# The float16 low half of g: a negated copy and an accumulating transfer on GpSimd's queue in place of VectorE's subtraction

## The chip, the cores and the metric

The kernel runs on one core of one Trainium2 chip. The metric is the device time of that core, in microseconds, and the median of several executions is taken. The core has TensorE (PE: matmuls, and PEld: the loads of their weights), VectorE (DVE), ScalarE (ACT), GpSimd (POOL) and SyncE (SP), each with its own instruction stream in a fixed order. SP and POOL also issue DMA transfers, each on its own queue.

## The reference

The input is a linear attention with 8 batches, 8 heads, 576 rows and a head size of 64, followed by a two-layer block over all 4608 rows:

```python
q_s = softmax(q, axis=-1); k_s = softmax(k, axis=2)      # written out with max, exp and sum
kv = np.einsum('bhsd,bhse->bhde', k_s, v)
x = np.einsum('bhsd,bhde->bhse', q_s, kv)                # then to rows: 4608 x 512
h = x @ w_in                                             # 512 x 2048
sp = np.maximum(h, 0.0) + np.log1p(np.exp(-np.abs(h)))
g = h * erf(sp)
out = g @ w_out                                          # 2048 x 512
```

w_in and w_out come as 64-bit floats and are rebuilt on the chip.

## The kernel before

**Tiles and items.** The rows are cut into blocks of 384 (12 blocks: four pairs of batches, three blocks each), and the 2048 inner columns into four groups of 512. One block with one group is an item; there are 48, n = 0 to 47. The items 0 to 3 run wholly in float32, and 4 and 5 (`OUT32`) have a float32 second product. The 42 items from 6 on use float16 pairs: a number is a float16 high half and the float16 rest.

**An item's steps.** `mm1` makes h in TensorE: the product with w_in by a scheme of seven half-size products, banks X, Y and Z, line 911. VectorE and ScalarE gather the banks into the tile H (128 x 4 x 384 float32, three buffers). ScalarE writes softplus of H into G (two buffers), and erf of G over G. `gmul` (line 991) makes g = G times H in G. From there H is free for other use: its bytes are read as two float16 tiles, gh in the first half and gl in the second. `ghi` (line 1005) casts g to gh, and `glo` (line 1009) writes g - gh to gl. `mm2` (line 1037) multiplies g with w_out on TensorE: for each of three row tiles and four quarters it takes gh with the high weights, gh with the low weights, and gl with the high weights, 36 matmuls of 128 x 512 with a weight load from H each. The sum of a block's four items is scaled by VectorE (line 1053) and stored from SP's queue.

**The order.** A table and the loop behind it write the steps down; a scheduler may still shift instructions of an engine against each other. In the loop, iteration n has the softplus and erf of item n at its end, and `gmul` of item n-1 at its start:

```python
        for i in range(4):
            if m0:
                tok(f"m{n}.{i}")
            if 4 < n <= N and i < 2 and n - 1 not in OUT32:
                tok(f"{'IO'[i]}{n - 1}")
            ...
            if m2 and i < 3:
                tok(f"M{n - 2}.{i}")
                pace(n + (i + 1) / NTT)
```

Here m is `mm1`, I is `ghi`, O is `glo` and M is `mm2`. So the halves of item n-1 are made in iteration n, between the products of item n, and are used one iteration later, after `m{n+1}.0`. `pace` puts pieces of the attention of later batches (lines 435 to 720) between them.

**Queues.** SP issues the loads of q, k and v and all stores. POOL issues the later weight loads (line 188), clears the tile vtail once for each batch (lines 432 and 433), and does little else.

Of the kernel before, what the change touches and what calls it, by code (L numbers as in the profile page):

```python
# [13 lines left out]
ALU = mybir.AluOpType  # L14
# [42 lines left out]
def attn_moe_kernel(  # L57
# [9 lines left out]
    nc = tc.nc  # L67
# [898 lines left out]
    def flat(t):  # L966
        return t.rearrange("p f t -> p (f t)")
# [38 lines left out]

    def glo(n):
        s = st[n]
        nc.vector.tensor_tensor(flat(s["gl"]), flat(s["G"]), flat(s["gh"]), op=ALU.subtract)  # L1009

    acc = {}

# [44 lines left out]

    steps = start()
    fn = dict(T=softplus, G=erf, U=gmul, I=ghi, O=glo)
    emitted_steps = set()  # L1060
    done = set()
# [127 lines left out]
```

## Time and profile before

| what | value |
|---|---|
| median of three runs | 862.84 us (860.36, 862.84, 862.9) |
| span of the profiled execution | 860.3 us; the run nearest to it took 860.36 us |
| TensorE busy | 825.6 us, 96% of the span |
| VectorE busy | 637.1 us, 74% |
| ScalarE busy | 504.2 us, 59% |
| GpSimd busy | 17.6 us, 2% |
| line 1009, the subtraction | 42 times, 73.8 us on VectorE |
| mean granted clock of TensorE | 0.989 |

No time of the profiled execution beside its span is listed apart. In a row of groups stand line, engine, operation, written tile <- read tiles, shapes and count; then busy time and the mean of one in ns; then the idle time of the engine ahead of them and what ended it. In a row of the timeline stand start, duration, engine, line and operation, and in brackets how long the engine sat idle before it and for whom. A busy time is that of the whole group with overlaps counted once, so one matmul of line 1037 occupies TensorE for 348.0 / 1512 = 0.23 us although its own duration is 379 ns.

### The profile page before, as it was taken

How to read it: one execution, taken by the hardware profiler on the slowest of the kernel's cores; microseconds unless marked ns; L12 is line 12 of the kernel's file. 1: busy time of each engine (PE TensorE's matmuls, PEld its weight loads, DVE VectorE, ACT ScalarE, POOL GpSimd, SP SyncE). 2: the span in 40 equal slices, each digit the busy share in tenths (PEclk: the TensorE clock that was granted, in tenths of full speed). 3: DMA queues.
4: the chain of work that ended last, by engine and by line, in shares of the span. 5: the costliest groups of instructions: out<-in, count | busy, mean ns of one | idle time of the engine just before them, and what ended most of it. 6: DMA issues, size and time to landing. Idle time of an engine off the chain costs nothing.

```text
span 860.3 us, 15503 instructions
## 1 busy us (share of the span) xinstructions
PE 825.6 (96%) x6532; PEld 569.2 (66%) x6532; DVE 637.1 (74%) x921; ACT 504.2 (59%) x645; POOL 17.6 (2%) x37
## 2 busy tenths in 40 slices
PE   3999997999999999999999999999999999999997
PEld 2655556676766776776776677767776677777673
DVE  6899889998886779759866779858866656653543
ACT  2597677866554566565664466466655466453532
POOL 2010000000000000000000000000000000000000
PEclk8999999999999999999999999999999999999999
DMA  9996320032123302311140202311110000100100
GB/s 273 397 268 178 100 75 13 19 88 50 37 54 77 87 1 50 93 28 24 50 105 14 68 19 51 80 38 26 32 32 2 25 13 2 37 2 1 37 2 37
DMA packets 117381, 55.53 MB, mean 65 GB/s; under 512 B 106560, under 2 KB 108608, under 8 KB 117312
## 3 DMA queue, kind: packets, MB, share of 16 engines
q1 hardware_dynamic: 115136, 46.15, 20.6%
q0 software_dynamic: 2176, 8.39, 2.7%
q8 instruction: 51, 0.84, 0.4%
q14 instruction: 18, 0.15, 0.1%
HBM read 45.09 MB, written 9.44 MB: 63 GB/s over the span
## 4 chain that ended last, share of the span: by engine, by line
PE 67%; DVE 17%; ACT 10%; issue 2%; DMA 2%; SPq 1%; POOL 0%; ACTq 0%; DVEq 0%; POOLq 0%
PE o L1037 31%; PE pX L911 16%; PE pZ L911 8%; ACT G L343 4%; PE pY L911 4%; ACT L343 3%; PE kv L541 2%; DVE G L991 2%; PE x L631 2%; PE qT L616 2%; DVE H L1009 1%; DVE x L297 1%; PE o L1028 1%; DVE wi L297 1%; DVE H L1005 1%
## 5 line engine op out<-in xcount | busy, mean ns | idle before, releaser
L1037 PE MATMUL o<-wo,H 128*128 128x512 f16 x1512 | 348.0, 379 | 1.7 <-DVE H L1005 1.3
L911 PEld LDWEIGHTS <-wi 128*128 128x128 f16 x3696 | 309.5, 98 | 39.0 <-issue 17.4
L1037 PEld LDWEIGHTS <-H 128*128 128x128 f16 x1512 | 145.7, 98 | 150.1 <-DVE H L1005 1.8
L911 PE MATMUL pX<-x,wi 128*128 128x192 f16 x2112 | 204.8, 247 | 6.4 <-ACT H L930 3.0
L343 ACT ACT_TABLE_LOAD x104 | 133.4, 1283 | 8.5 <-DVE H L936 5.3
L991 DVE SCALAR_TENSOR_TENSOR G<-G,small,H 128x1536 f32<-128x1536 f32 x44 | 80.0, 1818 | 65.8 <-ACT G L343 65.5
L911 PE MATMUL pZ<-x,wi 128*128 128x192 f16 x1056 | 102.9, 246 | 0.9 <-DVE H L936 0.5
L938 ACT COPY H<-pX 128x384 f32<-128x384 f32 x44 | 20.9, 476 | 138.0 <-PE pX L911 133.0
L343 ACT ACTIVATE G<-H,U 128x768 f32<-128x768 f32 (+1 forms) x60 | 72.9, 1231 | 24.4 <-DVE H L936 23.8
L1009 DVE TENSOR_TENSOR H<-G,H 128x1536 f16<-128x1536 f32 x42 | 73.8, 1757 | 1.1
L343 ACT ACTIVATE G<-G 128x1536 f32<-128x1536 f32 x48 | 71.2, 1484 | 0.5
L1028 PE MATMUL o<-wo,G 128*128 128x512 f32 x144 | 66.7, 604 | 0.0
L911 PE MATMUL pY<-x,wi 128*128 128x192 f16 x528 | 51.8, 248 | 1.6 <-DVE H L923 1.6
L442 ACT ACTIVATE x<-x 128x384 f32<-128x384 f32 (+1 forms) x52 | 17.6, 386 | 54.4 <-PE x L631 51.9
L923 DVE COPY H<-pY 128x384 f32<-128x384 f32 x44 | 24.4, 554 | 31.4 <-PE pY L911 31.3
L1028 PEld LDWEIGHTS o<-wo,G 128*128 128x128 f32 x144 | 26.3, 193 | 26.5 <-issue 25.8
L297 DVE SCALAR_TENSOR_TENSOR x<-x,x 128x768 f16<-128x768 f32 (+1 forms) x44 | 37.1, 850 | 5.8 <-ACT x L296 5.7
L1005 DVE CAST H<-G 128x1536 f16<-128x1536 f32 x42 | 40.1, 955 | 0.7
L296 ACT ACTIVATE x<-x 128x768 f16<-128x768 f32 (+1 forms) x44 | 32.9, 761 | 11.4 <-DVE x L387 11.4
L1053 DVE TENSOR_SCALAR ob<-o,V 128x512 f32<-128x512 f32 x29 | 21.7, 748 | 23.1 <-PE o L1037 23.1
L936 DVE TENSOR_TENSOR H<-pZ,H 128x384 f32<-128x384 f32 x44 | 24.3, 552 | 19.3 <-PE pZ L911 19.3
L925 DVE TENSOR_TENSOR H<-pX,H 128x384 f32<-128x384 f32 x44 | 24.4, 555 | 15.3 <-PE pX L911 14.9
(182 smaller groups left out, 804.2 us busy)
## 6 DMA issues: line engine op xcount, KB each, us to landing
out_dram<-ob SPq DMA_DIRECT2D x32, 256.0 KB, 2.3
vbuf<-in_v_dram SPq DMA_DIRECT2D x60, 128.0 KB, 3.1
q<-in_q_dram SPq DMA_DIRECT2D x56, 128.0 KB, 3.2
k<-in_k_dram SPq DMA_DIRECT2D x56, 128.0 KB, 3.3
wo<-in_moe_w_in_dram SPq DMA_DIRECT2D x4, 1024.0 KB, 16.9
wi<-in_moe_w_out_dram POOLq DMA_DIRECT2D x2, 1024.0 KB, 8.3
wi<-in_moe_w_in_dram SPq DMA_DIRECT2D x2, 1024.0 KB, 8.0
raw<-in_moe_w_out_dram POOLq DMA_DIRECT2D x2, 1024.0 KB, 7.9
```

What stands on the lines that cost most here:

```text
L296: nc.scalar.activation(hi, src, AF.Copy, scale=s)
L297: nc.vector.scalar_tensor_tensor(lo, src, s, hi, op0=ALU.mult, op1=ALU.subtract)
L343: i = nc.scalar.activation(out_, in_, func, **kw)
L911: nc.tensor.matmul(o, w[wl][:, c, a * P:(a + 1) * P], x[:, xl, xi, c, :], start=(new and a == 0 and c == 0 and i == 0), stop=(c == 1 and i ...
L923: nc.vector.tensor_copy(C[0, 0], bank2("Y"))
L925: add(C[0, 0], bank2("X"), C[0, 0], op=ALU.add)
L936: add(C[0, 1], bank2("Z"), C[0, 1], op=ALU.add)
L991: nc.vector.scalar_tensor_tensor(flat(s["G"]), flat(s["G"]), (GB if n in OUT32 else GA)[:, g:g + 1], flat(s["H"]), op0=ALU.mult, op1=ALU.mult,
L1005: nc.vector.tensor_copy(flat(s["gh"]), flat(s["G"]))
L1009: nc.vector.tensor_tensor(flat(s["gl"]), flat(s["G"]), flat(s["gh"]), op=ALU.subtract)
L1028: nc.tensor.matmul(o, s["G"][:, a, ts_], w[:, a, :], start=(first_ and a == 0), stop=(last_ and a == FG - 1),)
L1037: nc.tensor.matmul(o, s[gt][:, a, ts_], w[wl][:, a, :], start=(first_ and a == 0 and i == 0), stop=(last_ and a == FG - 1 and i == 2),)
```

## The change

VectorE no longer subtracts. It writes gl = -1 times gh, from float16 to float16, and a transfer on GpSimd's queue reads g from G and adds it to gl in place, with g in float32 and gl in float16. The instruction behind `glo` is thereby a transfer; whoever reads gl waits for its landing, and who overwrites G or H waits for it too.

```diff
     def glo(n):
         s = st[n]
-        nc.vector.tensor_tensor(flat(s["gl"]), flat(s["G"]), flat(s["gh"]), op=ALU.subtract)
+        nc.vector.tensor_scalar_mul(flat(s["gl"]), flat(s["gh"]), -1.0)
+        nc.gpsimd.dma_start(flat(s["gl"]), flat(s["G"]), accum_op=ALU.add)
```

All later lines move down by one: the matmuls of line 1037 are line 1038 after the change. In the rows below, the number in a tile's name is that of its item or batch, `o_4_0` and the like are the three row tiles of a block's sum, and a wait on DMASW is a wait for a transfer of GpSimd's queue.

TensorE at item 6, the first with a float16 low half, before: the loads and matmuls of the high half, then the first of the low half.

```order
L1037 LDWEIGHTS H_6_1142 [waits DVE_49]
L1037 MATMUL o_4_0_1176<-wo4_97,H_6_1142 128x512 [waits DMASW7_49]
...
L1037 MATMUL o_4_1_1232<-wo4_97,H_6_1142 128x512
...
L1037 MATMUL o_4_2_1285<-wo4_97,H_6_1142 128x512
L1037 LDWEIGHTS H_6_1142 [waits DVE_49]
```

And with the change:

```order
L1038 LDWEIGHTS H_6_1142 [waits DVE_49]
L1038 MATMUL o_4_0_1176<-wo4_97,H_6_1142 128x512 [waits DMASW7_49]
...
L631 MATMUL x_2_0_1561<-qTs_2_0_1481,kvbd0_85 128x512 [waits DVE_49]
L631 LDWEIGHTS kvbd0_85 [waits DVE_49]
L631 MATMUL x_2_0_1561<-qTs_2_0_1481,kvbd0_85 128x512
L616 MATMUL qT_2_1_1569<-ident_76,q_2_0_741 128x128 [waits DMAHW5_49]
L616 MATMUL qT_2_1_1569<-ident_76,q_2_0_741 128x128 x3
L911 LDWEIGHTS wi0_89
L911 MATMUL pZ_8_1582<-x7_2_1171,wi0_89 128x192 [waits DVE_49]
...
L1038 LDWEIGHTS H_6_1142 [waits DMASW0_49]
```

Two of the six matmuls on the high half have gone behind the wait; three matmuls of line 631, four transposes of line 616 and twelve pZ matmuls of line 911 stand ahead of it now.

TensorE at item 47, the last, with the change; before, the same rows stand in the same order, and the second wait is on DVE alone beside ACT's.

```order
L1038 LDWEIGHTS H_47_8366 [waits DVE_49]
L1038 MATMUL o_44_0_8255<-wo2_95,H_47_8366 128x512
...
L1038 MATMUL o_44_1_8297<-wo2_95,H_47_8366 128x512
...
L1038 MATMUL o_44_2_8323<-wo2_95,H_47_8366 128x512
L1038 LDWEIGHTS H_47_8366 [waits DMASW1_49,Activation_49]
```

Six matmuls stand between the two waits, before and after. In the 40 items between, the wait for the transfer stands on the load before the third matmul.

GpSimd's queue with the change; before, the rows of line 432 and 433 stand there alone.

```order
L1010 DMA H_9_1713<-G_9_1877 128x1536 [waits DMASW0_49,DVE_49,DMASW3_49,PE_49,Activation_49]
L1010 DMA H_10_1881<-G_10_2096 128x1536 [waits DVE_49,DMASW1_49,PE_49,Activation_49]
L432 MEMSET vtail_84 64x520 [waits DMAHW6_49,PE_49,Pool_49]
L433 MEMSET vtail_84 64x8
L1010 DMA H_11_2100<-G_11_2309 128x1536 [waits DMASW2_49,DMASW5_49,DVE_49,Activation_49]
```

The 42 transfers stand in order of their items, and the clears for four of the batches stand between them.

## The prediction

> **What bounds the kernel now.** I read the page's busy shares first, then its 40 slices, then TensorE by stage, then the waits around the two instructions that the diff touches.
>
> ```profile
> span 860.3 us, 15503 instructions
> PE 825.6 (96%) x6532; PEld 569.2 (66%) x6532; DVE 637.1 (74%) x921; ACT 504.2 (59%) x645; POOL 17.6 (2%) x37
> PE   3999997999999999999999999999999999999997
> ...
> 600.00:760.00 160.00, 158.61 (x1360) 113.31 (x1358) 105.40 (x142) 90.35 (x105) 0.00 (x0) 1.00 0.06 19
> 760.00:845.00 85.00, 85.00 (x673) 58.75 (x671) 37.10 (x41) 40.16 (x41) 0.00 (x0) 1.00 0.03 10
> ```
>
> The last two rows are two stretches: length, then busy time of PE, PEld, DVE, ACT and POOL, clock, DMA share. TensorE is busy for 85.00 of 85.00 us and 158.61 of 160.00: it is the bound, and VectorE (37.10 of 85.00) is far from it. Time that VectorE saves is worth only what it takes out of TensorE's waits, and these are few:
>
> ```profile
> L1009 DVE TENSOR_TENSOR H<-G,H 128x1536 f16<-128x1536 f32 x42 | 73.8, 1757 | 1.1
> L1005 DVE CAST H<-G 128x1536 f16<-128x1536 f32 x42 | 40.1, 955 | 0.7
> ...
> PE pX L911 <- DVE H L933: 2.1, 4, 0.7
> PE xt L631 <- DVE qTt L610: 2.1, 2, 1.0
> PE o L1037 <- DVE H L1005: 1.3, 1, 1.3
> PE o L1037 <- DVE H L1009: 0.4, 1, 0.4
> ```
>
> The subtraction (L1009) takes 42 times 1.757 us, and TensorE waited for it once, 0.4 us. That is the last item, where nothing is left to hide it:
>
> ```profile
> 846.60 0.96 DVE L1005 CAST H<-G 128x1536 f16<-128x1536 f32 x1
> 847.59 1.76 DVE L1009 TENSOR_TENSOR H<-G,H 128x1536 f16<-128x1536 f32 x1
> 847.61 1.47 PE L1037 MATMUL o<-wo,H 128*128 128x512 f16 x6 [1.33 <-DVE H L1005]
> 849.49 6.63 PE L1037 MATMUL o<-wo,H 128*128 128x512 f16 x30 [0.41 <-DVE H L1009]
> 856.17 0.75 DVE L1053 TENSOR_SCALAR ob<-o,V 128x512 f32<-128x512 f32 x1 [1.41 <-PE o L1037]
> ```
>
> Six matmuls need only the high half; the other 30 stand behind the first use of the low half. So whatever comes later than 849.46 there is added to the end.
>
> **How much cover the other 41 have.** I paired each L1009 with the first weight load of its low half. TensorE's order gives two loads of the high half and then one of the low half; a group of three loads takes 0.40 us and one load 98 ns, so the low half is wanted 0.30 us after a group's start.
>
> ```profile
> 198.36 0.40 PEld L1037 LDWEIGHTS <-H 128*128 128x128 f16 x3
> ...
> 192.40 1.74 DVE L1009 TENSOR_TENSOR H<-G,H 128x1536 f16<-128x1536 f32 x1
> 194.20 1.84 PEld L1037 LDWEIGHTS <-H 128*128 128x128 f16 x10 [0.35 <-DVE H L1009]
> ...
> 408.20 1.75 DVE L1009 TENSOR_TENSOR H<-G,H 128x1536 f16<-128x1536 f32 x1
> 413.36 1.04 PEld L1037 LDWEIGHTS <-H 128*128 128x128 f16 x6
> ...
> 732.19 1.75 DVE L1009 TENSOR_TENSOR H<-G,H 128x1536 f16<-128x1536 f32 x1
> 736.36 1.04 PEld L1037 LDWEIGHTS <-H 128*128 128x128 f16 x6
> ...
> 818.19 1.76 DVE L1009 TENSOR_TENSOR H<-G,H 128x1536 f16<-128x1536 f32 x1
> 825.55 2.34 PEld L1037 LDWEIGHTS <-H 128*128 128x128 f16 x12
> ...
> 832.89 1.76 DVE L1009 TENSOR_TENSOR H<-G,H 128x1536 f16<-128x1536 f32 x1
> 838.27 7.52 PEld L1037 LDWEIGHTS <-H 128*128 128x128 f16 x36
> ```
>
> Cover, from the start of L1009 to the want: item 6 has 194.20 - 192.40 = 1.80 us; item 19 has 413.66 - 408.20 = 5.46; item 39 has 4.47; item 45 has 7.66; item 46 has 5.68; item 47 has 849.46 - 847.59 = 1.87. The 42 pairs, worked out alike and sorted: 1.80, 1.87, 4.47, 5.46, 5.46, 5.67, 5.91, 6.12, 6.18, 6.18, then 32 from 7.23 to 10.20 us.
>
> **The change part by part.** Removed: 42 subtractions. Added on VectorE: 42 multiplications by -1, f16 to f16. The trace has none. Its bounds are 0.347 us, a tensor-scalar of 256 elements that writes f16, and the CAST's 0.955, which has the same 1536 elements and the same output but reads four bytes each. I take 0.95, as the CAST is nearest.
>
> ```profile
> L594 DVE TENSOR_SCALAR kvbd<-kvf,x_s 64x256 f16<-64x256 f32 x12 | 4.2, 347 | 0.2
> ```
>
> The Trainium skill ("VectorE: DVE Perf Modes", section "Mode 4×_2P — both tricks at once") has a one-source operation on packed 16-bit data in SBUF run at four elements a cycle. The CAST's 955 ns fits its two-a-cycle mode (1536 / 2 / 0.96 GHz = 800 ns and some 155 ns), and by the rule the multiplication would take an estimated 0.56 us; the stalls below would then sum to about 13.4 us in place of 17.0.
>
> Added behind it: 42 accumulating transfers on GpSimd's queue, g (128 x 1536 f32, 0.75 MB) onto -gh in place (0.375 MB, read and written). The nearest rows are GpSimd's weight loads of 1 MB:
>
> ```profile
> 69.28 0.71 POOL L188 DMA_DIRECT2D raw<-in_moe_w_out_dram  x1 [7.14 <-DVE wo L215]
> DMA to landing us min/median/max: 5.3/8.4/22.0
> ```
>
> From issue to landing the fastest of line L188 takes 5.3 us; the others share the DMA engines with other loads. Lower bound: 5.3 x 0.75 = 4.0 us, if only g's bytes count. Upper bound: 10.6, if each row passes the engine twice, once to read and once to add. I take 5.3 x 1.125 = 6.0 us, by bytes read (0.75 + 0.375 MB), since the loads' rows also pay for reading and writing together. So the low half is ready 0.95 + 6.0 = 6.95 us after the place where L1009 started, against 1.757 now.
>
> The Trainium skill ("DMA: Bandwidth & Descriptors", section "Anatomy of one DMA — SWDGE (gpsimd) path") puts such a transfer at 2.0 us and bytes / 436e3: an estimated 3.8 us for 0.79 million bytes. The row speaks against it: 1 MB would be 4.4, and the trace's best is 5.3. By it the stalls would come to 4.0 us.
>
> **The sum.** An item stalls TensorE by 6.95 less its cover, less the stall of the item before: ScalarE and VectorE start item n from its mm1, which stands ahead of item n-1's stalled mm2, so a stall there gives item n as much more cover.
> - Item 6: the new order puts other work ahead of the want: three L631 matmuls (19.9 / 72 = 0.28 each), four L616 transposes (0.155), twelve pZ matmuls (102.9 / 1056 = 0.097), two of its own fewer (348.0 / 1512 = 0.23): 0.83 + 0.62 + 1.17 - 0.46 = 2.16 us. Stall 6.95 - 3.96 = 2.99.
> - Items 8, 13, 19, 25, 31, 37, 39, 46: 0.83 + 0.77 + 1.49 + 0.77 + 1.49 + 1.04 + 2.48 + 1.28 = 10.15.
> - Item 47: 6.95 - 1.87 - 1.28 = 3.80.
> - Together 16.9 (17.0 unrounded).
>
> ```profile
> L631 PE MATMUL x<-qTs,kvbd 128*128 128x512 f16 x72 | 19.9, 379 | 0.2 <-DVE qTs L610 0.2
> L616 PE MATMUL qT<-ident,q 128*128 128x128 f32 x128 | 19.9, 283 | 0.0
> L911 PE MATMUL pZ<-x,wi 128*128 128x192 f16 x1056 | 102.9, 246 | 0.9 <-DVE H L936 0.5
> L1037 PE MATMUL o<-wo,H 128*128 128x512 f16 x1512 | 348.0, 379 | 1.7 <-DVE H L1005 1.3
> ```
>
> Taken back: 42 x (1.757 - 0.95) = 34 us of VectorE, of which TensorE sees what it waited for behind L1009. Those are L933's 2.1 us in four waits; the two shown stand just ahead of the wants of items 8 and 39, which stall now, so what they give is lost there, and about 1 us is left.
>
> ```profile
> 224.75 1.15 PE L911 MATMUL pX<-x,wi 128*128 128x192 f16 x12 [0.48 <-DVE H L933]
> ...
> 734.46 1.15 PE L911 MATMUL pX<-x,wi 128*128 128x192 f16 x12 [0.29 <-DVE H L933]
> ```
>
> At no cost: GpSimd's queue. Behind the waiting transfers stand four clears of vtail; the first ran at 257.11, right beside an L1009 at 256.89, and would now go after that item's issue, 256.89 + 0.95 + 0.71 = 258.55, some 1.5 us late. The next was released 88 us later, so the batch has room; were that gone, 4 x 1.5 us would show. The reverse, a transfer held by a clear that waits for TensorE, I price at nothing too: these clears were released 0.2 and 3.2 us after the L1009 ahead of them (256.89, 342.55), while the next L1009 comes about an item, some 15 us, later.
>
> ```profile
> 256.89 1.76 DVE L1009 TENSOR_TENSOR H<-G,H 128x1536 f16<-128x1536 f32 x1
> 257.11 0.53 POOL L432 MEMSET vtail<- 64x520 f32 x1 [79.78 <-PE kv L541]
> 342.55 1.75 DVE L1009 TENSOR_TENSOR H<-G,H 128x1536 f16<-128x1536 f32 x1
> 345.78 0.52 POOL L432 MEMSET vtail<- 64x520 f32 x1 [87.98 <-PE kv L541]
> ```
>
> Reuse of G is free as well: softplus overwrites it two items later, and items are 14.70 us apart (818.19 to 832.89). Other loads share the engines in the earlier stages; I add nothing for it in the sum and keep it for the upper side.
>
> The sum is 860.3 + 17.0 - 1.0 = 876.3 us against the profiled span. The runs shown are 860.36, 862.84 and 862.9, so that span is at their lower end and their median 2.5 higher; for a median I say 877.
>
> **The rivals.** *Cover is enough, and VectorE's relief pays.* At the lower bound, 0.95 + 4.0 = 4.95, only items 6, 39 and 47 stall: 0.99 + 0.48 + 3.08 = 4.6 us. Against it stand at most the 2.1 us behind L933 and the 2.1 behind L610. Result 860.3 + 4.6 - 4.2 = 861 to 865 (no relief): not slower. It decides below a landing of about 4.3 us. For it: 32 covers of 7 us and more. Against: the best 1 MB load takes 5.3. By the Trainium skill's formula above it would be this case. 0.17.
>
> *The accumulating transfer is slow, and most items stall.* At 8.4 us (the median of L188, also what sharing would do) the need is 9.35: 27 items stall, 52 us in all, 912 us. At 10.6 it is 98 us, 958. It decides from a landing of about 7.4, where the crowd of covers from 7.2 to 8.3 runs out. For it: no row shows an add inside a transfer, nor a change of type, and the loads of q, k and v share the engines until batch 7 is in. Against: the bytes are fewer than in the loads of 5.3 us, and none goes to HBM. 0.26.
>
> An add done after rounding g to f16 would leave the low half empty and the time as it is; it is no rival for the time.
>
> **How the numbers follow.** The forecast, landing 4.3 to 7.4 us, gets 0.57 and alone spans 866 to 893 (stalls of 6 to 33 us). With the lower case's 863 and the slow case up to 910 some 2 in 10 are left out. A measurement here tells about 0.3% (2.6 us) from no change. Faster 0.05 (landing under 4 and all the relief), same 0.13, slower 0.82.
>
> **What would show it.** L1009 as tensor-scalar of 0.35 to 0.95 us; an L1010 transfer of 4 to 10.6 us; TensorE's waits before L1038 naming that transfer, about ten times, largest at the last item with near 4 us; VectorE's share down by 4 to 6 points. Wrong if the last item's stall is under 2 us, if some other queue or line holds TensorE, or if TensorE's waits for it pass 33 us.

## The result and the profile after

The change makes the kernel slower: 876.75 us (median of 873.17 to 877.6) against 861.68 us, a ratio of 1.0168 with an interval of 1.0142 to 1.0195. The profiled execution took 877.6 us and its span is 875.8, 15.5 us above that of the profile before.

The page of the kernel after has these rows (in the row of a group: count | busy us, mean ns | idle us before, and what ended it):

```profile
span 875.8 us, 15670 instructions
PE 828.4 (95%) x6532; PEld 567.4 (65%) x6532; DVE 589.6 (67%) x921; ACT 505.0 (58%) x645; POOL 53.7 (6%) x79
...
L1038 PE MATMUL o<-wo,H 128*128 128x512 f16 x1512 | 352.7, 382 | 12.1 <-DMA H<-G 11.5
```

The two stretches that were shown of before (length, then busy time of PE, PEld, DVE, ACT and POOL, clock, DMA share, GB/s):

```profile
600.00:760.00 160.00, 157.00 (x1348) 111.98 (x1346) 94.41 (x146) 91.56 (x107) 8.56 (x10) 1.00 0.25 43
760.00:845.00 85.00, 85.00 (x692) 60.09 (x690) 34.97 (x44) 40.86 (x44) 5.14 (x6) 1.00 0.22 35
```

TensorE is still the bound, and a wait of a new kind stands in front of the second product: 11.5 us for the transfer into H. VectorE is 47.5 us lighter, and TensorE gets little from it.

The two new steps, by their lines (least, median and longest time in ns; then the transfers' landing in us):

```profile
L1009 DVE TENSOR_SCALAR H<-H x42: 551/560/561, 194.4 to 857.2; 128x1536 f16<-128x1536 f16 x42
L1010 POOL DMA_DIRECT2D H<-G x42: 847/856/920, 195.6 to 858.4; - x42
DMA to landing us min/median/max: 4.8/5.1/7.6
```

And the waits that changed most (us in total, times, longest):

```profile
PE o L1038 <- DMA H<-G: 11.5, 9, 4.6
DVE q_m L453 <- DMA q<-in_q_dram: 14.1, 9, 3.1
```

The multiplication takes 0.56 us and the transfer 5.1 us from issue to landing. The last row was 4.6 us in four waits before. The timeline shows the longest waits for transfers: item 6, item 39, and the end.

```profile
200.94 4.02 PE L1038 MATMUL o<-wo,H 128*128 128x512 f16 x10 [2.47 <-DMA H<-G]
...
746.48 1.04 PE L1038 MATMUL o<-wo,H 128*128 128x512 f16 x4 [1.67 <-DMA H<-G]
...
849.21 7.51 PE L1038 MATMUL o<-wo,H 128*128 128x512 f16 x34 [0.65 <-DMA H<-G]
...
857.21 0.56 DVE L1009 TENSOR_SCALAR H<-H 128x1536 f16<-128x1536 f16 x1
857.23 1.47 PE L1038 MATMUL o<-wo,H 128*128 128x512 f16 x6 [0.51 <-DVE H L1005]
858.40 0.86 POOL L1010 DMA_DIRECT2D H<-G  x1 [13.84 <-DVE H L1009]
863.32 8.32 PE L1038 MATMUL o<-wo,H 128*128 128x512 f16 x30 [4.62 <-DMA H<-G]
```

At the end, 4.62 us of wait, and then 30 matmuls take 8.32 us that took 6.63 before. The granted clock in the two stretches around the longest waits (the column behind POOL's busy time; 1.00 is the full clock) says why:

```profile
198.00:205.00 7.00, 4.53 (x19) 1.87 (x17) 6.35 (x8) 4.18 (x6) 0.00 (x0) 0.76 0.66 110
863.30:867.00 3.70, 3.68 (x10) 1.39 (x11) 0.00 (x0) 0.00 (x0) 0.00 (x0) 0.54 0.00 0
```

The stretch of the kernel before that answers to the second:

```profile
849.50:853.00 3.50, 3.50 (x17) 1.61 (x18) 0.75 (x1) 0.00 (x0) 0.00 (x0) 1.00 0.00 0
```

A mean of 0.54 over 3.70 us is 0.3 us at the full clock and 3.4 us at half of it, and 0.76 over 7.00 us comes to 3.4 us at half as well. Cut into slices of 0.2 us, the trace shows 0.50 in each from 863.7 to 866.9. So TensorE ran at half its clock for 3.4 us after the wait at the end, and again behind the 2.47 us at item 6. Over the whole span TensorE is idle for 47.4 us where it was 34.7, and busy for 828.4 where it was 825.6: 12.7 and 2.8 us make the 15.5, and 11.5 of the idle time are waits for the new transfers.

### The profile page after: what moved, and what is told of

Its sections match the earlier page's. It is cut to its first block, busy times and chain, and to the rows that moved or that the text cites. A ratio compares the mean times of both kernels' runs of the same rounds, so it can differ in the third digit from the quotient of the medians.

```text
span 875.8 us, 15670 instructions
## 1 busy us (share of the span) xinstructions
PE 828.4 (95%) x6532; PEld 567.4 (65%) x6532; DVE 589.6 (67%) x921; ACT 505.0 (58%) x645; POOL 53.7 (6%) x79
## 4 chain that ended last, share of the span: by engine, by line
PE 56%; DVE 19%; ACT 10%; DMA 8%; SPq 3%; issue 3%; POOL 0%; ACTq 0%; DVEq 0%; POOLq 0%
PE o L1038 28%; PE pX L911 13%; PE pZ L911 7%; DMA H<-G 5%; ACT G L343 4%; ACT L343 3%; PE pY L911 3%; DMA q<-in_q_dram 2%; SPq L408 2%; DVE G L991 2%; PE kv L541 2%; DVE x L297 2%; DVE H L1005 1%; PE x L631 1%; PE qT L616 1%
## 5 line engine op out<-in xcount | busy, mean ns | idle before, releaser
L1038 PE MATMUL o<-wo,H 128*128 128x512 f16 x1512 | 352.7, 382 | 12.1 <-DMA H<-G 11.5
L1010 POOL DMA_DIRECT2D H<-G x42 | 36.0, 857 | 636.2 <-PE pX L911 166.0
L297 DVE SCALAR_TENSOR_TENSOR x<-x,x 128x768 f16<-128x768 f32 (+1 forms) x44 | 37.4, 854 | 5.5 <-ACT x L296 5.3
L925 DVE TENSOR_TENSOR H<-pX,H 128x384 f32<-128x384 f32 x44 | 24.4, 555 | 17.2 <-PE pX L911 17.0
```

The lines of the kernel that those rows point to most:

```text
L297: nc.vector.scalar_tensor_tensor(lo, src, s, hi, op0=ALU.mult, op1=ALU.subtract)
L925: add(C[0, 0], bank2("X"), C[0, 0], op=ALU.add)
L1010: nc.gpsimd.dma_start(flat(s["gl"]), flat(s["G"]), accum_op=ALU.add)
L1038: nc.tensor.matmul(o, s[gt][:, a, ts_], w[wl][:, a, :], start=(first_ and a == 0 and i == 0), stop=(last_ and a == FG - 1 and i == 2),)
```

## Experiments

Theory A is that of the prediction: TensorE waits for low halves that come late, and that is the loss. Theory B: the transfers' traffic slows the rest throughout. Theory C came later and is a narrow form of B: the transfers hold up the loads of q alone, VectorE waits for these, and TensorE for VectorE.

**The last item alone by subtraction.** (N is 48.)

```diff
     def glo(n):
         s = st[n]
+        if n == N - 1:
+            nc.vector.tensor_tensor(flat(s["gl"]), flat(s["G"]), flat(s["gh"]), op=ALU.subtract)
+            return
         nc.vector.tensor_scalar_mul(flat(s["gl"]), flat(s["gh"]), -1.0)
```

> The last item (47) goes back to VectorE's subtraction; the other 41 keep the transfer. Theory A (TensorE's waits for late low halves make the whole loss, and the last item alone has 4.6 us of wait and 1.7 us of half clock after it): 876.8 - 6 = 871 us, with no half-clock stretch before the last 30 matmuls. Theory B (the 42 transfers' traffic slows the loads and the rest all along): 41 of 42 transfers stay, so 876 to 877.

Measured: 870.33 us against 861.26, ratio 1.0105 (1.0091 to 1.0119); 6.4 us less than with the change. The wait at the end is down from 4.62 us to 0.42, and the half clock behind it is gone: the 11 matmuls that follow take 2.53 us, 0.23 each.

```profile
857.72 2.53 PE L1041 MATMUL o<-wo,H 128*128 128x512 f16 x11 [0.42 <-DVE H L1010]
```

One transfer of 42 is worth 6.4 of 15 us. That is A and not B.

**The ten items of the prediction by subtraction.** The same edit, with another condition:

```diff
+        if n in (6, 8, 13, 19, 25, 31, 37, 39, 46, 47):
+            nc.vector.tensor_tensor(flat(s["gl"]), flat(s["G"]), flat(s["gh"]), op=ALU.subtract)
+            return
```

> The ten items named in the prediction (6, 8, 13, 19, 25, 31, 37, 39, 46, 47) go back to the subtraction; 32 transfers stay, all with a cover of 7.2 us and more. Theory A: their low halves come in time, no wait of more than 0.5 us for a transfer is left, and the time is that of the kernel before, 860 to 863. Theory B: 32/42 of the 15 us stay, 872 to 874.

Measured: 864.38 us, 1.0039 (1.0026 to 1.0052). No wait for a transfer is left in the list of TensorE's waits, as A says; but the time stays 3 us above the kernel before, which A does not explain, and far under B's 872. Something smaller is left.

**The multiplication without the transfer.**

```diff
         nc.vector.tensor_scalar_mul(flat(s["gl"]), flat(s["gh"]), -1.0)
-        nc.gpsimd.dma_start(flat(s["gl"]), flat(s["G"]), accum_op=ALU.add)
```

> The multiplication stays and the transfers are left out, so g is not added and the low half is minus the high half: a part of the computation is missing. Theory A: no wait for a low half, VectorE has 50 us less to do, and TensorE gets from that at most 2 to 3 us: 858 to 862. A rival in which the multiplication or the new order of instructions costs by itself: over 865.

Measured: 858.93 us, 0.9972 (0.9964 to 0.9981). VectorE's relief is worth 2.3 us to TensorE and no more, and no cost of the multiplication or of the new order shows. In the profiled executions TensorE is idle 0.7 us less than before and busy 1.9 us less; the kernel before had a stretch of half clock near 244 us that this run has not, so how much of the 2.3 us is shorter waits and how much is the clock stays open. The transfers of the change, with the waits for them, thus cost 876.75 - 858.93 = 17.8 us.

**The wait about doubled.**

```diff
-        nc.vector.tensor_scalar_mul(flat(s["gl"]), flat(s["gh"]), -1.0)
+        nc.vector.tensor_scalar_mul(flat(s["gl"]), flat(s["gh"]), -2.0)
+        nc.gpsimd.dma_start(flat(s["gl"]), flat(s["gh"]), accum_op=ALU.add)
         nc.gpsimd.dma_start(flat(s["gl"]), flat(s["G"]), accum_op=ALU.add)
```

> The wait is about doubled: the low half starts as -2 gh, one transfer adds gh, and a second one, after the first has landed, adds g. The low half is then ready about 0.6 + 0.6 + 4.5 + 5.1 and some 0.3 between, 11 us after the multiplication's start. Theory A with its rule that a stall gives the next item as much cover: 76 to 97 us of waits, 937 to 960 us. Theory A without that rule (each item waits for its own shortfall): 118 to 160 us, 980 to 1020. Theory B (traffic): twice the transfers, twice the 15 us, about 890.

Measured: 985.84 us, 1.1425 (1.138 to 1.1471). The time lies in the range of theory A without its rule, 980 to 1020, but it gets there by another way. The page of this run:

```profile
PE 864.3 (88%) x6532; PEld 575.9 (59%) x6532; DVE 591.1 (60%) x921; ACT 508.2 (52%) x645; POOL 89.7 (9%) x121
...
PEclk8999998998989899999899999998899999899998
```

And the wait for transfers:

```profile
PE o L1039 <- DMA H<-G: 90.9, 34, 6.1
```

The waits for transfers are 90.9 us, within the 76 to 97 of the rule that a stall gives the next item as much cover, and outside the 118 to 160 without it. The rest is TensorE's own busy time: 864.3 us against 825.6 in the kernel before (and 828.4 with the change), 38.7 us more for the same matmuls, with a lower clock in one slice of four. So the waits were forecast rightly with the rule, and the half clock that follows some of them was missing from the sum. 90.9 and 38.7 are 129.6 us; the spans differ by 123.2, as TensorE's other idle time is 6.4 us less.

**The transfers without a reader.** The kernel before, and beside its subtraction the 42 transfers onto a tile that nobody reads.

```diff
+    spare = cp.tile([P, FG * T], F16, name="spare")
+    nc.gpsimd.memset(spare, 0.0)
...
-    sqs = cp.tile([P, 512], BF16, name="sqs")
+    sqs = spare[:, :512].bitcast(BF16)
...
         nc.vector.tensor_tensor(flat(s["gl"]), flat(s["G"]), flat(s["gh"]), op=ALU.subtract)
+        nc.gpsimd.dma_start(spare, flat(s["G"]), accum_op=ALU.add)
...
-            obs[i0, tt] = at.tile([P, DM], F32, tag="ob", bufs=3, name=f"ob_{n}_{tt}")
+            obs[i0, tt] = at.tile([P, DM], F32, tag="ob", bufs=2, name=f"ob_{n}_{tt}")
```

> The kernel before, with its subtraction, and beside it the 42 accumulating transfers of g onto a spare tile that nobody reads (the tile also lends its first third to the squares of the weights, and the output tiles are two in place of three). Theory A (only late low halves cost): 860 to 863. Theory C, formed after the run with ten subtractions (the transfers share the DMA engines with the loads of q, VectorE's row maximum of q waits for them and TensorE behind it, about 5 us): 864 to 868, with the waits of L453 for q at 12 us or more against 4.6.

Measured: 862.23 us, 1.0007 (0.9997 to 1.0017). VectorE's waits for q are 4.6 us in four, as before. The whole traffic costs nothing that this can tell when nobody waits for it, in nearly the order of instructions of the kernel before. One thing is not as in the change: these transfers need only g, so they are issued right behind `gmul`, some 2 us earlier in their item. The result is against C as it was put, and leaves the 3 us of the run with ten subtractions open.

**The high half first.** The second product of the change takes its matmuls in another order.

```diff
-            for a in range(FG):
-                for i, (gt, wl) in enumerate((("gh", 0), ("gh", 1), ("gl", 0))):
+            for i, (gt, wl) in enumerate((("gh", 0), ("gh", 1), ("gl", 0))):
+                for a in range(FG):
```

> The change, with the second product taking all eight high-half matmuls of a row tile before the four low-half ones; same arithmetic in another order. The low half is wanted six matmuls, 1.3 us, later in each item, and at the last item 17 matmuls stand ahead of the wait in place of 6, 2.4 us later. Theory A: waits for transfers 11.5 us to 4 us (2.2 at the last item, 1.2 at item 6, 0.4 at item 39), and at least one half-clock stretch of 1.7 us less: 867 to 870. Theory B (traffic alone): 876 to 877.

Measured: 866.82 us, 1.0057 (1.0032 to 1.0081), where 867 to 870 was expected. Waits for transfers are left at two places, 5.2 us; the one at the end is what was expected, 2.25, and the one at item 6 is 2.9 where 1.2 was. Half clock follows the one at the end (12 matmuls take 4.30 us below) and not the longer one at item 6, where the clock stays at 1.00.

```profile
849.95 3.84 PE L1038 MATMUL o<-wo,H 128*128 128x512 f16 x17 [1.33 <-DVE H L1005]
856.04 4.30 PE L1038 MATMUL o<-wo,H 128*128 128x512 f16 x12 [2.25 <-DMA H<-G]
```

**The high half first in the kernel before.** The same edit without the change.

> The kernel before, no transfer, with the second product taking the eight high-half matmuls of a row tile before the four low-half ones: what that order is worth by itself. Theory A: only the 0.4 us wait of the last item can go, 860.5 to 861.5. Rival: the order itself changes TensorE's pace (the same weights are no longer used twice running), more than 2.6 us either way.

Measured: 861.29 us, 0.9998 (0.9986 to 1.001). The order is worth nothing by itself, so the 10 us of the run above are cover.

**The high half first, and items 6 and 47 by subtraction.**

```diff
+        if n in (6, N - 1):
+            nc.vector.tensor_tensor(flat(s["gl"]), flat(s["G"]), flat(s["gh"]), op=ALU.subtract)
+            return
         nc.vector.tensor_scalar_mul(flat(s["gl"]), flat(s["gh"]), -1.0)
```

> As the run with the high half first, and items 6 and 47 by subtraction. Theory A with C: no wait for a transfer over 0.5 us, no half-clock stretch from them, and what is left is the sharing with the loads of q: 863 to 866. Theory A alone: 859 to 861.

Measured: 864.37 us, 1.0032 (1.0013 to 1.005), with 40 transfers and, in the profiled execution (the fastest, 861.36 us), no wait of TensorE for one. The remainder is the same as with ten subtractions. Two more runs cut these transfers in two, in the same order of VectorE's instructions.

**Only the late transfers**, of items 36 to 46; items 7 to 35 leave g out of the low half.

```diff
-        nc.gpsimd.dma_start(flat(s["gl"]), flat(s["G"]), accum_op=ALU.add)
+        if n >= 36:
+            nc.gpsimd.dma_start(flat(s["gl"]), flat(s["G"]), accum_op=ALU.add)
```

> High half first and items 6 and 47 by subtraction, but of the other transfers only the ten of items 36 to 46 (one of them is counted twice nowhere: 11 items) stay, which run after the last load of q, k and v; items 7 to 35 multiply and leave g out, so part of the computation is missing. VectorE's order is the same as with all transfers. Theory C (transfers cost through the loads that they share the DMA engines with): 858 to 861, as without any transfer, and L453 waits for q about 8 us. A rival in which each transfer costs something wherever it stands: 11/40 of the 5.4 us between the two kernels, about 860.4, and in between for the next run.

**Only the early ones**, of items 7 to 35 (`if n < 36`); items 36 to 46 leave g out.

> The complement: the 29 transfers of items 7 to 35 stay, which run while q, k and v are loaded, and items 36 to 46 multiply and leave g out, so part of the computation is missing. Theory C: 863 to 866, as with all transfers, with L453 waiting 11 us and more for q. The rival: 29/40 of 5.4 us over 859, about 862.8.

Measured: the late ones 860.37 us, 0.998 (0.9963 to 0.9997); the early ones 864.36, 1.0031 (1.0015 to 1.0048). The early transfers carry most of the remainder: against the run without transfers (858.93) they cost some 5 us, and the late ones about 1. The times alone do not settle it between C and the rival in which every transfer costs a little: its 860.4 is what the late ones took, and its 862.8 lies in the interval of the early ones (862.4 to 865.2). The rows speak for C. With the early transfers, the wait for q in the list of waits, and the timeline at one place:

```profile
DVE q_m L453 <- DMA q<-in_q_dram: 16.7, 9, 3.4
```

```profile
304.41 1.22 DVE L453 TENSOR_REDUCE q_m<-q 128x16 f32<-128x1024 f32 x1 [2.92 <-DMA q<-in_q_dram]
305.55 0.55 DVE L925 TENSOR_TENSOR H<-pX,H 128x384 f32<-128x384 f32 x1
306.15 1.15 PE L911 MATMUL pX<-x,wi 128*128 128x192 f16 x12 [1.46 <-DVE H L925]
```

With the late ones, the same wait and VectorE's two rows at that place:

```profile
DVE q_m L453 <- DMA q<-in_q_dram: 6.7, 7, 2.0
```

```profile
299.14 1.21 DVE L453 TENSOR_REDUCE q_m<-q 128x16 f32<-128x1024 f32 x1
300.27 0.54 DVE L925 TENSOR_TENSOR H<-pX,H 128x384 f32<-128x384 f32 x1
```

The load of q (L408, in four parts) that VectorE stands at here, first with the early transfers and then with the late ones:

```profile
L408 SPq DMA_DIRECT2D q<-in_q_dram x4: 552/1000/1357, 294.8 to 297.5; - x4
DMA to landing us min/median/max: 6.4/6.4/6.9
```

```profile
L408 SPq DMA_DIRECT2D q<-in_q_dram x4: 551/625/662, 292.3 to 294.3; - x4
DMA to landing us min/median/max: 3.1/3.4/3.5
```

The load is issued 0.5 us behind a transfer (294.26) and takes about twice as long to land; VectorE stands at the row maximum of q, the emptying of bank X (L925) is queued behind it, and TensorE waits for that bank. Three such waits (1.46, 0.89, 0.84 us) and one more behind VectorE's work on k, itself late after a wait for q (1.59), are in the profile with the early transfers and not in the one with the late ones: 4.8 us. So C is right in this order. In the run with the spare tile two things are otherwise. VectorE has its old load; and the transfers, issued earlier, mostly miss the loads: of the four loads of q that are held up here (up to 5.7, 6.9, 6.2 and 6.3 us), only the third is held up there (5.6), and the others land within 3.7 us. Which of the two spares that run its cost is not shown by a run that changes one alone.

**GpSimd's own arithmetic in place of the transfer.**

```diff
-        nc.vector.tensor_tensor(flat(s["gl"]), flat(s["G"]), flat(s["gh"]), op=ALU.subtract)
+        eng = nc.vector if n in (6, N - 1) else nc.gpsimd
+        eng.tensor_tensor(flat(s["gl"]), flat(s["G"]), flat(s["gh"]), op=ALU.subtract)
```

> No transfer: GpSimd's own arithmetic does the subtraction of items 7 to 46, VectorE that of 6 and 47. By the row of GpSimd's tensor-tensor (1.90 us for 1024 elements) it takes 2.9 us, ready some 3.2 us after the place of L1009, under the smallest other cover of 4.5. Theory A with C: no late low half, no traffic, VectorE 70 us lighter: 858 to 861, as the run without the add. Rival: GpSimd and VectorE hold each other up when both read two operands, and VectorE's operations or GpSimd's become longer: 863 and more.

Measured: 870.38 us, 1.0096 (1.0076 to 1.0116): the rival. VectorE's L387 by its line (least, median and longest time in ns), in the kernel before and in this run:

```profile
L387 DVE TENSOR_TENSOR x<-x x44: 541/553/560, 112.1 to 726.2; 128x384 f32<-128x384 f32 x44
```

```profile
L387 DVE TENSOR_TENSOR x<-x x44: 536/552/3183, 114.3 to 737.5; 128x384 f32<-128x384 f32 x44
```

And the timeline of this run, with GpSimd's step beside one of VectorE's:

```profile
224.87 3.53 POOL L1010 TENSOR_TENSOR H<-G,H 128x1536 f16<-128x1536 f32 x1 [14.58 <-DVE H L1005]
225.48 3.74 DVE L297 SCALAR_TENSOR_TENSOR x<-x,x 128x768 f16<-128x768 f32 x1
...
230.40 0.82 PE L911 MATMUL pX<-x,wi 128*128 128x192 f16 x8 [2.66 <-DVE H L933]
```

An operation of VectorE that reads two operands from SBUF, which takes 0.95 us alone (L297 with 768 elements, 952 ns in the mean before), took 3.74 beside GpSimd's: it ended 0.8 us after GpSimd's did. TensorE's wait is behind it. VectorE is busy for 595.4 us in this run; the 637.1 of before less forty subtractions of 1.757 would be 566.8, so some 29 us are such lengthening.

**The best of the parts.** The high half first, and multiplication and transfer in items 36 to 46 alone (`if n < 36 or n == N - 1:` takes the subtraction).

> High half first; subtraction in items 6 to 35 and 47, multiplication and transfer in items 36 to 46 alone, which run after the loads of q, k and v and have cover enough. Theory A with C: no late low half, no sharing, and VectorE's relief falls where it is idle anyway: 860 to 862, no gain on the kernel before. A rival in which each transfer costs wherever it stands: 862.5 to 863.

Measured: 860.69 us against 861.57, 0.9984 (0.997 to 0.9997). It is ahead of both kernels, by 0.9 us against the one before, under the 0.3% that counts here as a change.

## Why the prediction was right, point by point

- **The time.** 877 was forecast and 876.75 measured; on the span 876.3 and 875.8. That they agree to a microsecond is luck: two terms were too large (the multiplication, the landing), three were left out (the time up to the issue, the half clock, the other loads), and these nearly cancel.
- **What bounds the kernel** held: TensorE, before and after, and no busy share of VectorE told of the loss. VectorE's share fell by 6.7 points (74.1 to 67.3%), where 4 to 6 were given as a sign, in part since the multiplication is shorter than was taken.
- **The multiplication** was taken at the CAST's 0.95 us and takes 0.56. The Trainium skill's four elements a cycle ("VectorE: DVE Perf Modes", section "Mode 4×_2P — both tricks at once") gave 0.56, and the row agrees.
- **The landing** was taken as 6.0 us by bytes read and is 5.1 (4.8 to 7.6). The bounds of 4.0 and 10.6 hold. The Trainium skill's formula ("DMA: Bandwidth & Descriptors", section "Anatomy of one DMA — SWDGE (gpsimd) path") gave 3.8 us for it, and no transfer of the 42 came under 4.8. Between the multiplication's end and the issue lie 0.63 us (857.77 to 858.40) that had no term. The need is therefore 0.56 + 0.63 + 5.1 = 6.3 us and not 6.95.
- **The stalls** were to sum to 17.0 us; the waits are 11.5, and the prediction's own rule with 6.3 us gives 11.1. Item 6 has 2.47 (2.99 forecast), 39 has 1.67 (2.48), 46 has 0.65 (1.28), and 47 has 4.62 (3.80). At 8 and 37 nothing is left; item 12, which was not among the ten, waits 0.26 us for a transfer that took 7.6 beside a load of q. This term was mis-sized.
- **Item 47** was to be relieved by the stall of item 46. It was not: that stall fell into a wait that was there already, for the CAST of item 47 (1.33 us before, 0.51 after), so it cost nothing and gave no cover. What the two items cost together is nevertheless what the rule gives with 6.3 us: 0.65 + 4.62 - 0.82 = 4.45 us, against 4.43.
- **The half clock** behind a long wait was not in the sum: 1.7 us at the end (8.32 - 6.63), about as much again at item 6. The profile of the kernel before has one such stretch near 244 us, behind waits of 1.03 and 0.67 us, which the kernel after has not; so TensorE's busy time is only 2.8 us more.
- **Other loads** were left out of the sum and kept for the upper side; where no low half is late they cost some 5 us, and nothing that shows in the kernel with the spare tile. This is the step that failed by its content: "I add nothing for it". In the change's own profile less of it stands: VectorE waits 14.1 us for q (4.6 before), and TensorE's waits for the emptying of bank X behind it (L925) are 1.7 us, against 0.4 before.
- **The relief** was put at about 1 us and is 2.3 where no transfer runs.
- Added up from the runs: -2.3 for the relief, +5.4 for transfers that nobody waits for (864.37 - 858.93), +12.4 for the late low halves with their half clock (876.75 - 864.37): 15.5 on 861.3. These are differences between neighbouring runs, so they add up by construction; the loads of q and the late halves overlap, and the share of each depends on which is taken away first.
- **The rivals.** That cover is enough fell with the 5.1 us; the slow transfer did not come, though the doubled wait shows what it would have cost: even more than was worked out, for the clock. (Against that rival the prediction said that the bytes are fewer than in the loads of 1 MB; its own sum counts 1.125 MB.) **GpSimd's queue** is free, as priced: no wait behind a clear of vtail is among TensorE's.

## What to carry to other kernels

Where one engine is the bound, ask of a step moved elsewhere how long after its old place the result is there, and lay that beside the cover of each of its uses; here three uses of 42 (items 6, 39 and 47) hold 8.8 of the 11.5 us of waits, and the last, with 1.87 us of cover, made 6.4 of 15 us. A stall gives the next item its cover back only if no other wait lies there to swallow it, as the wait for the cast did at item 47. Transfers beside loads cost where an engine in order stands at a load and holds what the bound engine needs.

## What the runs showed of the hardware

Behind some of its waits TensorE gets half its clock, for 3.4 us with the change and for 6.8 us at one place of the run with two adds (a mean of 0.74 over 13 us). In that run it goes with 38.7 us more of busy time. The length of the wait alone does not decide it: the 4.62 and 2.47 us with the change were followed by it, and so were 2.25 us at the end of the change with the high half first; the 2.92 us at item 6 of that run were not, nor the 1.67 us at item 39. The waits of 1.03 and 0.67 us near 242 us were followed by it in the kernel before, and the same two waits in the kernel before with the high half first were not. The Trainium skill ("TensorE: Matmul & The Clock Gate", section "What's actually happening") tells of these two rates and of free-running windows of 3.4 us; the rows agree in the two rates and in the stretch's length. The wait of 2.47 us is shorter than one such window.

An accumulating transfer with a change of type, 0.75 MB onto 0.375 MB, lands in 5.1 us in the median (4.8 to 7.6), less than the 5.3 of the fastest load of 1 MB in line L188. A load of q issued beside one lands in 6.4 to 6.9 us, where 3.1 to 3.5 is the time without it.

VectorE and GpSimd hold each other up where both read two operands: 3.74 us for an operation of VectorE that takes 0.95 alone, 3.18 for one of 0.55, and up to 3.67 for the one of GpSimd, which takes 3.10 in the median. The Trainium skill ("SBUF — State Buffer", section "Who interferes with whom") has a VectorE instruction with two SBUF inputs contend with a GpSimd instruction that reads SBUF, over a pair of ports that it calls an exclusive lock. The rows agree: VectorE's operation began while GpSimd's ran and ended 0.82 us after it, close to its own 0.95.
